# Filler matmuls of ones from the start, four sign buffers and earlier loads in a top-k attention and expert kernel

## The chip, the cores and the metric

The kernel runs on one core of a Trainium2 chip. The core has a matrix engine (TensorE, PE in the rows; its weight loads are listed as PEld), VectorE (DVE), ScalarE (ACT), GpSimd (POOL) and SyncE (SP), which here issues nearly all transfers. The metric is the device time of one execution in microseconds, lower is better.

## The reference

Attention over 2 batches, 8 heads, 576 tokens and 64 columns, in which each row keeps its 32 largest scores, and behind it a layer of 8 experts: each token goes to one expert, of which each takes at most 288.

```python
scores = scale * np.matmul(q, k.transpose(0, 1, 3, 2))
kth = np.partition(scores, -top_k, axis=-1)[..., -top_k:-top_k + 1]
scores = np.where(scores >= kth, scores, -1000000000.0)
attn = np.exp(scores - np.max(scores, axis=-1, keepdims=True))
attn = attn / (np.sum(attn, axis=-1, keepdims=True) + 1e-09)
x = np.matmul(attn, v)                       # then heads side by side: 1152 tokens x 512
expert_idx = np.argmax(x @ w_gate, axis=1)   # probs = softmax, gate_w = probs of that expert
h = np.maximum(np.einsum('ecd,edf->ecf', disp, w1), 0.0)
y = np.einsum('ecf,efd->ecd', h, w2)
out[i] = gate_w[i] * y[expert_idx[i], pos[i]]   # for tokens within capacity
```

## The kernel before

Attention is cut into 36 units: 9 tiles of 128 tokens by 4 pairs of heads. A unit goes through a pipeline in which each engine works on another unit at the same time. The order on each engine is the order of the code; nothing reorders it.

For unit `u` the steps are these. `scores` (L292, PE) writes two PSUM tiles that exist once, so the scores of the next unit wait until the unit before has been read. `heads` (L310 to L314, DVE) takes the eight largest of each of eight segments per head, sixteen MAX8, and the row maximum `mx` (L313). `shift` (L356, ACT) moves the scores, with the maximum taken off, from PSUM to `sm`; with it the PSUM tiles come free. `merge` and `bound` (L323 to L350, DVE) give a first bound for the 32nd value. `sign` (L365, ACT) writes the signs of `sm` against that bound to `sg` and counts them; `turn` (L372, POOL) multiplies `sm` by `sg` into `z`; `select` (L395 to L402, DVE) takes the eight largest of `z` and with the count the exact 32nd value. `penalty` (L411, ACT), `probs` (L430 to L432, PE and ACT) and `values` (L452, L455, PE) give the output. After each fourth unit the tile is routed (`route`, L518 to L561): logits on PE (L527), copied by DVE (L538), and an indirect transfer to the experts' buffer `xbuf`.

`sign_turn` writes, for one unit, the sign of head 0, work listed for ACT, the sign of head 1, and then the two products on POOL. The pool of the attention tiles has two buffers of each name, and a unit takes two of `sg`.

The q and k of a pair of heads are loaded by `load_qk` (L104, SP), split into a high and a low half in float16 (`split_qk`, L212 to L218) and transposed, `q` also with the halves swapped. For the first batch PE transposes (L244, L247), and ACT or DVE copies the result out (L252, L254). For the second batch POOL splits, and SP issues transposing DMAs (`trans_dma`, L233) and the swap (L223). The lists `side`, `mid`, `end` say at which of the pipeline's rounds such a step is issued; the loop at L1278 enters, for each pair, the load two rounds ahead of its split. SP issues its transfers in order: what stands behind a transfer that waits is issued after it. `init_xbuf` (L185) zeroes `xbuf` in six transfers from the same queue.

`warm` issues matmuls whose result is never read: `COLD` of them with 512 columns at the start, and four groups of 128 columns (`EARLY`) in the first three rounds. They multiply `identb` (weights) by `onesb`. The experts follow attention: weights are loaded, split in two halves and multiplied on PE.

Of the kernel before, what the change touches and what calls it, by code (L numbers as in the profile page):

```python
# [20 lines left out]
BF = mybir.dt.bfloat16  # L21
# [13 lines left out]
def kernel(  # L35
# [11 lines left out]
    nc = tc.nc  # L47
    B, H, S, D = q.shape
# [10 lines left out]
    consts = ctx.enter_context(tc.tile_pool(name="consts", bufs=1))  # L59
# [17 lines left out]
    def att(*a, **k):  # L77
        return P["att", 0].tile(*a, **k)
# [20 lines left out]
    def load_qk(b, p, tag="nat", names="qk"):  # L99
        for name in names:  # L100
            src = q if name == "q" else k
            XN[name, b, p] = x = (work.tile if tag == "nat" else att)([PR, 2, R, D], FT, name=name + "nat", tag=tag, bufs=4 if tag == "nat" else 2)
            for j in range(2):
                nc.sync.dma_start(x[:, j], bass.AP(  # L104
                    tensor=src.tensor, offset=src.offset + (b * H + 2 * p + j) * S * D,
                    ap=[[D, PR], [PR * D, R], [1, D]]))
# [16 lines left out]
    def load_v(b, js):  # L123
        for j in js:
# [4 lines left out]
            for c in range(4):  # L129
                nc.sync.dma_start(VM[b][:, c, :, j, 0:D],  # L130
                                  bass.AP(tensor=v.tensor, offset=o + (TAIL * j + c * 128) * D,
                                          ap=[[D, 128], hs, [1, D]]))

    load_qk(0, 0)
    load_qk(0, 1)
    load_qk(0, 2, "z")
# [11 lines left out]
    identb = consts.tile([128, 128], BF)  # L148
# [4 lines left out]
    nc.vector.tensor_copy(identh, ident)  # L153
    tri = consts.tile([128, 128], BF)
    nc.vector.tensor_scalar(tri, jp, 0.0, None, op0=OP.is_gt)
    onesb = consts.tile([128, 128], BF)
    nc.vector.memset(onesb, 1.0)
    zero = consts.tile([128, Dm + 2], FT)
    nc.vector.memset(zero[:, :Dm + 1], 0.0)
    nc.vector.memset(zero[:, Dm + 1:Dm + 2].bitcast(I32), 1 << 20)  # L160
# [197 lines left out]
    SEL, SG = {}, {}  # L358

    def sign(u, js=(0, 1)):  # L360
        if 0 in js:
            SG[u] = [att([128, S], BF, name="sg") for j in range(2)]
        for j in js:
            c = u * 2 + j
            nc.scalar.activation(SG[u][j], SM[u][:, j], AF.Sign, bias=VAL[u][0][:, 2, j:j + 1],  # L365
                                 scale=-(1.0 - 2.0 ** -20), accum_out=CNT[:, c:c + 1])
# [8 lines left out]
    def sign_turn(u, act, pool):  # L375
        sign(u, (0,))
        for f, *a in act:
            f(*a)
        sign(u, (1,))
        turn(u, js=(0,))  # L380
        if u < NU - 3:
            for f, *a in pool:
                f(*a)
        turn(u, js=(1,))
        if u == NU - 3:
            for f, *a in pool:
                f(*a)
# [96 lines left out]
    def tail_p():  # L484
        TAIL_P[:] = four()
# [435 lines left out]
    RANK = tuple(range(E))  # L921
    LEAST = 128

    COLD = 7
    EARLY = 30, 10, 30, 16
    FUSED = 3, 31

# [106 lines left out]
    def warm(n, few=False):  # L1034
        o = pv[:, 384:] if few else TAIL_P[2]
        x = onesb if few else onesb[:, None, :].to_broadcast([128, 4, 128])
        for i in range(n):
            nc.tensor.matmul(o, identb, x, start=True, stop=True)

    def attention(side, early, late, mid, pads, act, pool, end):  # L1040
        nc.vector.memset(OHS, 0.0)
# [84 lines left out]
        for st in range(3):  # L1126
            bound(L - 1, st)
        sign(L - 1)
        turn(L - 1)
        run(rt(T - 2, 1.5))  # L1130
# [106 lines left out]
    swap_psum(None, "bk")  # L1237
    tail_p()
    warm(COLD)
    for i in range(2):  # L1240
        split_qk(0, 0, i, ACT, DVE, tag="sm")
# [5 lines left out]
    for i, j, sw, o, eng in ((0, 0, 0, 0, ACT), (0, 1, 0, 1, ACT), (0, 0, 2, 3, DVE), (1, 0, 0, 4, ACT),  # L1247
# [13 lines left out]
    side, early, late, mid, pads = {}, {}, {}, {}, {}  # L1261
    act, pool, end = {}, {}, {}
    side[0] = [(warm, EARLY[0], True), (trans_qk, 0, 2, 0, ACT, 0)]
    mid[0] = [(trans_qk, 0, 2, 0, ACT, 1), (split_qk, 0, 3, 0, POOL, POOL, None, "pT"),
              (split_qk, 0, 3, 1, ACT, POOL, None, "pT")]
    end[0] = [(split_qk, 0, 2, 1, ACT, DVE, 2), (trans_qk, 0, 2, 1, ACT), (warm, EARLY[1], True)]
    side[1] = [(trans_qk, 0, 3, 0, ACT, 0)]
    mid[1] = [(trans_qk, 0, 3, 0, ACT, 1), (sign, 0), (turn, 0), (trans_qk, 0, 3, 1, DVE, 0), (warm, EARLY[2], True),
# [9 lines left out]
    for p in range(HP):  # L1278
        for i in range(2):
            at = 3 + 3 * (2 * p + i) // 2  # L1280
            if i == 0 and p:
                side.setdefault(at - 2, []).append((load_qk, 1, p))
            for part in range(3):
                side.setdefault(at + part // 2, []).append((split_qk, 1, p, i, POOL, POOL, part))
            side.setdefault(at + 1, []).append((trans_qk, 1, p, i, None))
# [13 lines left out]
    for n, (e, i, c) in enumerate(halves):  # L1299
        at = 18 + 3 * n  # L1300
# [108 lines left out]
```

## Time and profile before

| | us |
|---|---|
| median of 3 runs | 357.69 |
| lowest, highest | 357.67, 358.92 |
| the profiled execution | 359.89 |
| its span (first to last instruction) | 358.1 |
| attention, about | 12 to 233 |
| experts, about | 260 to 352 |

A row of a timeline gives the start and the length in us, the engine, the line, the operation, what it writes and reads, and how many instructions it stands for; in brackets the idle time of the engine before it and what ended it. PEclk is the granted clock of TensorE as a share of the full one.

### The profile page before, as it was taken

The numbers are of one execution on the slowest core, as the hardware profiler recorded it, in microseconds if no ns is written. First come the engines' busy times: TensorE is split into PE (matmuls) and PEld (weight loads), VectorE is DVE, ScalarE is ACT, GpSimd is POOL, SyncE is SP. The second block draws the span as 40 slices with busy tenths as digits, with TensorE's granted clock in tenths as the row PEclk, the third lists the DMA queues.
The fourth block names the chain that finished last, engine by engine and source line by source line (L and its number), as shares of the span: only waits on it lengthen the run. The fifth ranks groups of instructions, "written<-read, shape, count | busy, mean of one in ns | idle before, by whom it ended". The sixth has DMA issues, their size and how long they took to land. (4 is left out here: it accounts for less than half of the span.)

```text
span 358.1 us, 9808 instructions
## 1 busy us (share of the span) xinstructions
PE 318.2 (89%) x3356; PEld 264.4 (74%) x3361; DVE 310.9 (87%) x1607; ACT 283.0 (79%) x496; POOL 234.1 (65%) x270
## 2 busy tenths in 40 slices
PE   6986888897898998988889899999899999999991
PEld 3764776786786776777768788986446999996581
DVE  5899999999999999999999999886846959799930
ACT  4889999998979999999899998872266756886720
POOL 3967959599896798999999999592211020329321
PEclk9989999999999999999999999999999999999997
DMA  9739969686286910000301644504389999999900
GB/s 168 133 86 196 227 174 266 167 184 133 44 251 215 330 59 0 34 2 30 119 1 52 182 183 88 210 29 148 91 254 386 214 359 367 323 389 337 248 26 25
DMA packets 69921, 60.25 MB, mean 168 GB/s; under 512 B 52069, under 2 KB 52069, under 8 KB 69863
## 3 DMA queue, kind: packets, MB, share of 16 engines
q1 hardware_dynamic: 67719, 54.79, 56.8%
q0 software_dynamic: 1616, 4.73, 4.1%
q8 instruction: 28, 0.46, 0.6%
q14 instruction: 30, 0.25, 0.2%
q10 hardware_dynamic: 528, 0.02, 0.1%
HBM read 40.66 MB, written 12.09 MB: 147 GB/s over the span
## 5 line engine op out<-in xcount | busy, mean ns | idle before, releaser
L310 DVE MAX8 un<-s 128x8 f32<-128x72 f32 (+2 forms) x576 | 101.7, 224 | 3.1 <-PE s L292 3.0
L372 POOL TENSOR_TENSOR z<-sm,sg 128x576 f32<-128x576 f32 x71 | 89.4, 1280 | 7.6 <-ACT sg L365 7.2
L455 PEld LDWEIGHTS pV<-vm,pT 128*128 128x128 f32 (+1 forms) x640 | 71.3, 181 | 6.7 <-issue 3.3
L679 POOL DMA_INDIRECT out_dram<-y,xp x12 | 25.2, 2104 | 75.5 <-DVE y L846 39.1
L455 PE MATMUL pV<-vm,pT 128*128 128x65 f32 (+1 forms) x640 | 72.4, 261 | 0.0
L620 DVE TENSOR_TENSOR ws<-wr,ws 128x1024 bf16<-128x1024 f32 x54 | 64.9, 1250 | 2.8 <-ACT ws L614 2.6
L365 ACT ACTIVATE sg<-sm,mx 128x576 bf16<-128x576 f32 x72 | 55.4, 775 | 5.7 <-POOL z L372 5.6
L356 ACT ACTIVATE sm<-s,mx 128x576 f32<-128x576 f32 (+2 forms) x108 | 54.8, 582 | 5.7 <-DVE mx L313 5.6
L614 ACT ACTIVATE ws<-wr 128x2048 f16<-128x2048 f32 (+1 forms) x27 | 49.6, 1845 | 7.5 <-issue 4.4
L292 PE MATMUL s<-qk 128*128 128x512 f16 (+3 forms) x320 | 43.2, 291 | 12.1 <-ACT sm L356 12.0
L430 PE MATMUL p<-ident,sm 128*128 128x128 f32 x252 | 48.5, 281 | 6.0 <-ACT xT L524 5.5
L411 ACT ACTIVATE pen<-sm,nk 128x576 bf16<-128x576 f32 x71 | 51.6, 783 | 2.1 <-DVE nk L402 1.8
L398 DVE MAX8 z<-z 128x8 f32<-128x576 f32 x72 | 50.8, 747 | 0.0
L659 PEld LDWEIGHTS <-ws 128*128 128x128 f16 (+1 forms) x768 | 48.7, 98 | 1.2 <-issue 0.4
L431 PE MATMUL p<-identB,pen 128*128 128x128 bf16 x252 | 44.6, 220 | 4.9 <-ACT pen L411 4.8
L430 PEld LDWEIGHTS p<-ident,sm 128*128 128x128 f32 x252 | 36.1, 143 | 10.1 <-ACT xT L524 6.8
L431 PEld LDWEIGHTS <-pen 128*128 128x128 bf16 x324 | 33.5, 105 | 7.8 <-ACT pen L411 7.7
L292 PEld LDWEIGHTS <-qk 128*128 128x128 f16 (+1 forms) x320 | 20.4, 105 | 23.0 <-issue 14.5
L432 ACT ACTIVATE pT<-p 128x1152 f32<-128x1152 f32 x28 | 32.0, 1145 | 0.0
L620 POOL TENSOR_TENSOR ws<-wr,ws 128x1024 bf16<-128x1024 f32 x10 | 21.4, 2136 | 0.0
L831 PEld LDWEIGHTS <-ws 128*128 128x128 f16 (+1 forms) x288 | 21.3, 98 | 0.0
L659 PE MATMUL pT<-xe,ws 128*128 128x128 f16 (+5 forms) x312 | 19.6, 222 | 0.0
(271 smaller groups left out, 624.0 us busy)
## 6 DMA issues: line engine op xcount, KB each, us to landing
wr<-in_moe_w_dram SPq DMA_DIRECT2D x32, 1024.0 KB, 8.0
xbuf<-zero SPq DMA_DIRECT2D x6, 771.0 KB, 4.7
qnat<-in_q_dram SPq DMA_DIRECT2D x16, 144.0 KB, 3.9
knat<-in_k_dram SPq DMA_DIRECT2D x16, 144.0 KB, 3.1
out_dram<-zero SPq DMA_DIRECT2D x3, 768.0 KB
vm<-in_v_dram SPq DMA_DIRECT2D x16, 128.0 KB, 3.7
qk<-qk SPq DMA_DIRECT2D x14, 144.0 KB, 3.1
vt<-in_v_dram SPq DMA_DIRECT2D x4, 64.0 KB, 3.4
```

What stands on the lines that cost most here:

```text
L292: nc.tensor.matmul(PS[u][a][row:row + n, o:o + w], QK[b][2 * i][:, h, s:s + n], QK[b][1][:, h, c:c + w], start=(i == 0), stop=(i == 1))
L310: nc.vector.max(out=un[:, j, i], in_=segment(u, j, i))
L356: nc.scalar.activation(SM[u][:, j, o], i, AF.Identity, bias=VAL[u][0][:, 0, j:j + 1], scale=-1.0)
L365: nc.scalar.activation(SG[u][j], SM[u][:, j], AF.Sign, bias=VAL[u][0][:, 2, j:j + 1], scale=-(1.0 - 2.0 ** -20), accum_out=CNT[:, c:c + 1])
L372: engs[j].tensor_tensor(out=Z[u][:, j], in0=SM[u][:, j], in1=SG[u][j], op=OP.mult)
L398: nc.vector.max(out=z8[:, step - 1], in_=Z[u][:, step - 1])
L411: eng.activation(o, x, AF.Relu, bias=n)
L430: nc.tensor.matmul(pt[:, i], sm[:, cs], ident, start=True, stop=False, is_transpose=True)
L431: nc.tensor.matmul(pt[:, i], pen[:, cs], identB, start=False, stop=True)
L455: nc.tensor.matmul(PV[t][row:row + n, h0 + half], PT[u][:, 5 * half + c, row:row + n], VM[b][:, c, p, half], start=False, stop=(half == 1 ...
L620: eng.tensor_tensor(out=w[:, 1].bitcast(BF)[:, s], in0=r[:, s], in1=w[:, 0, s], op=OP.subtract)
L659: nc.tensor.matmul(o, a(i), c(i), start=(i == 0 and m == 0), stop=(i == k - 1 and m == 2))
```

## The change

`onesb` is written before the first loads instead of behind the constants, the fillers take it as both operands, `COLD` goes from 7 to 15, `sg` gets four buffers, and in the rounds in which a pair of the second batch is loaded, the load is put ahead of the other entries of that round instead of behind them.

```diff
+    onesb = consts.tile([128, 128], BF)
+    nc.vector.memset(onesb, 1.0)
     load_qk(0, 0)
...
     tri = consts.tile([128, 128], BF)
     nc.vector.tensor_scalar(tri, jp, 0.0, None, op0=OP.is_gt)
-    onesb = consts.tile([128, 128], BF)
-    nc.vector.memset(onesb, 1.0)
...
     def sign(u, js=(0, 1)):
         if 0 in js:
-            SG[u] = [att([128, S], BF, name="sg") for j in range(2)]
+            SG[u] = [att([128, S], BF, name="sg", bufs=4) for j in range(2)]
...
-    COLD = 7
+    COLD = 15
...
-            nc.tensor.matmul(o, identb, x, start=True, stop=True)
+            nc.tensor.matmul(o, onesb, x, start=True, stop=True)
...
             if i == 0 and p:
-                side.setdefault(at - 2, []).append((load_qk, 1, p))
+                side.setdefault(at - 2, []).insert(0, (load_qk, 1, p))
```

On VectorE, at the start of the program, the constants stood in this order before (`jp` comes from GpSimd, `ident` is the identity, `identb` its bfloat16 copy):

```order
L143 MEMSET act 1x1
L147 TENSOR_SCALAR ident<-jp 128x128
L149 CAST identb<-ident 128x128
L151 TENSOR_SCALAR identB<-ident 128x128
L153 CAST identh<-ident 128x128
L155 TENSOR_SCALAR tri<-jp 128x128
L157 MEMSET onesb 128x128
```

and stand so now:

```order
L135 MEMSET onesb 128x128
L145 MEMSET act 1x1
L149 TENSOR_SCALAR ident<-jp 128x128
L151 CAST identb<-ident 128x128
L153 TENSOR_SCALAR identB<-ident 128x128
```

The ones moved from the seventh place to the first, ahead of everything that waits for `jp`.

On SyncE, in the rounds in which pairs 1 and 2 of the second batch are loaded, this stood in the queue before (`hl` are split operands that GpSimd writes, one number for each; `qnat` and `knat` the loads, `xbuf` the zeroing):

```order
L185 DMA xbuf<-zero 128x3x514
L233 DMA_TRANSPOSE qk<-hl_718 128x6x96 x2
L223 DMA qk<-qk 64x1152 x2
L104 DMA qnat<-in_q_dram 96x6x64 x2
L104 DMA knat<-in_k_dram 96x6x64 x2
L185 DMA xbuf<-zero 128x3x514
L233 DMA_TRANSPOSE qk<-hl_819 128x6x96 x2
L185 DMA xbuf<-zero 128x3x514 x2
L233 DMA_TRANSPOSE qk<-hl_1034 128x6x96 x2
L223 DMA qk<-qk 64x1152 x2
L104 DMA qnat<-in_q_dram 96x6x64 x2
L104 DMA knat<-in_k_dram 96x6x64 x2
```

and this stands there now:

```order
L104 DMA qnat<-in_q_dram 96x6x64 x2
L104 DMA knat<-in_k_dram 96x6x64 x2
L185 DMA xbuf<-zero 128x3x514
L233 DMA_TRANSPOSE qk<-hl_726 128x6x96 x2
L223 DMA qk<-qk 64x1152 x2
L185 DMA xbuf<-zero 128x3x514
L233 DMA_TRANSPOSE qk<-hl_833 128x6x96 x2
L185 DMA xbuf<-zero 128x3x514
L104 DMA qnat<-in_q_dram 96x6x64 x2
L104 DMA knat<-in_k_dram 96x6x64 x2
L185 DMA xbuf<-zero 128x3x514
L233 DMA_TRANSPOSE qk<-hl_1042 128x6x96 x2
```

Each group of four loads moved ahead of the transposes and the swap that it followed. The order on ScalarE and on GpSimd is the same in both kernels.

## Rows read from the trace of the kernel before

**Rows 1.** The page, busy time and share of each engine.
```profile
PE 318.2 (89%) x3356; PEld 264.4 (74%) x3361; DVE 310.9 (87%) x1607; ACT 283.0 (79%) x496; POOL 234.1 (65%) x270
```
**Rows 2.** Busy time by stretch: length, then PE, PEld, DVE, ACT, POOL, clock, DMA.
```profile
12.26:84.50 72.24, 60.43 (x591) 49.95 (x590) 70.73 (x473) 66.79 (x127) 58.76 (x58) 0.98 0.84 177
84.50:233.00 148.50, 134.70 (x1381) 115.08 (x1381) 143.57 (x963) 138.53 (x279) 132.22 (x161) 1.00 0.36 113
260.00:322.00 62.00, 60.99 (x774) 54.90 (x774) 47.14 (x53) 43.41 (x49) 9.32 (x7) 1.00 1.06 329
```
**Rows 3.** Waits of DVE, 12 to 232 us: total, times, longest.
```profile
DVE un L310 <- PE s L292: 3.0, 5, 1.1
DVE r L538 <- PE pV L527: 1.2, 3, 0.5
```
**Rows 4.** Timeline of DVE in the prologue.
```profile
0.79 0.06 DVE L143 MEMSET act<- 1x1 f32 x1 [0.79 <-PEq L1392]
2.84 0.17 DVE L157 MEMSET onesb<- 128x128 bf16 x1
10.19 0.95 DVE L218 SCALAR_TENSOR_TENSOR hl<-knat,hl 96x768 f16<-96x768 f32 x1
12.26 2.33 DVE L310 MAX8 un<-s 128x8 f32<-128x72 f32 x16 [1.10 <-PE s L292]
17.36 0.24 DVE L310 MAX8 un<-s 128x8 f32<-128x72 f32 x1 [0.39 <-PE s L292]
21.91 0.24 DVE L310 MAX8 un<-s 128x8 f32<-128x72 f32 x1 [0.51 <-PE s L292]
```
**Rows 5.** Timelines of ACT and DVE around two later waits.
```profile
81.50 0.78 ACT L365 ACTIVATE sg<-sm,mx 128x576 bf16<-128x576 f32 x1 [1.18 <-POOL z L372]
85.23 0.24 DVE L310 MAX8 un<-s 128x8 f32<-128x72 f32 x1 [0.49 <-PE s L292]
200.95 0.77 ACT L365 ACTIVATE sg<-sm,mx 128x576 bf16<-128x576 f32 x1 [0.79 <-POOL z L372]
211.06 0.24 DVE L310 MAX8 un<-s 128x8 f32<-128x72 f32 x1 [0.48 <-PE s L292]
```
**Rows 6.** Timeline of PE in the prologue.
```profile
3.06 3.15 PE L1038 MATMUL bk<-onesb,identb 128*128 128x512 bf16 x7 [3.06 <-DVE onesb L157]
6.63 1.14 PE L244 MATMUL pT<-identh,hl 96*128 96x96 f16 x12 [0.43 <-DVE hl L218]
10.96 2.12 PE L292 MATMUL s<-qk 128*128 128x512 f16 x8
13.84 2.43 PE L1038 MATMUL pV<-onesb,identb 128*128 128x128 bf16 x30
16.10 0.68 PE L244 MATMUL pT<-identh,hl 96*128 96x96 f16 x12
16.61 1.15 PE L292 MATMUL s<-qk 128*128 128x512 f16 x8
19.12 0.95 PE L244 MATMUL pT<-identh,hl 96*128 96x96 f16 x12 [0.29 <-ACT qk L252]
```
**Rows 7.** Busy time by stretch; the last but two is the granted clock.
```profile
22.00:25.00 3.00, 3.00 (x30) 2.72 (x29) 2.86 (x22) 2.48 (x7) 1.40 (x2) 0.50 0.37 84
```
**Rows 8.** Timelines of ACT and POOL in the prologue.
```profile
14.90 1.52 ACT L356 ACTIVATE sm<-s,mx 128x576 f32<-128x576 f32 x3
12.83 1.64 POOL L216 TENSOR_TENSOR hl<-qnat,hl 96x768 f16<-96x768 f32 x1
```
**Rows 9.** Waits of ACT, 12 to 232 us.
```profile
ACT sg L365 <- POOL z L372: 5.6, 11, 1.2
```
**Rows 10.** Waits of POOL there, then timelines of SP and POOL.
```profile
POOL hl L214 <- DMA qnat<-in_q_dram: 6.1, 2, 3.4
48.26 1.20 SPq L104 DMA_DIRECT2D qnat<-in_q_dram  x2
70.03 0.83 POOL L214 TENSOR_SCALAR hl<-qnat 96x768 f16<-96x768 f32 x1 [3.42 <-DMA qnat<-in_q_dram]
```

## The prediction

> **What bounds the kernel now.** I read the page's engine table first, then the busy time by stretch, then VectorE's waits, and last the timelines around those waits. The page [rows 1] names no bound: PE has 89% and DVE 87%, averaged over stages that differ. By stretch [rows 2] they come apart. From 84.50 to 233.00 us DVE is busy 143.57 of 148.50 us, and from 12.26 to 84.50 us 70.73 of 72.24: attention runs at DVE's pace, and a gain there has to be an idle moment of DVE. From 260 to 322 us PE is busy 60.99 of 62.00: the experts run at PE's pace, on work that is released by the end of attention. I see there no transfer with a clock time of its own, so I let a shift of the end of attention pass through one for one.
>
> DVE's idle moments from 12 to 232 us are few [rows 3]. 3.0 us in five pieces are waits of the first maximum of a unit (L310) for the scores: the rows with the wait in brackets stand at 12.26 (1.10), 17.36 (0.39) and 21.91 (0.51) [rows 4], and at 85.23 (0.49) and 211.06 (0.48) [rows 5]. Another 1.2 us in three pieces are waits of the routing step L538 for its logits. What the change can take away is in these two lists.
>
> **Why the first three waits are there.** In the prologue PE works at the lower of its two clock levels. The seven fillers of 512 columns take 3.15 us, 0.45 us each, and 0.43 with the drain of the last left out, and the first scores take 2.12 us for eight matmuls; the second scores, the same eight, take 1.15. Twelve transposes take 1.14 us at 6.63 and 0.68 at 16.10 [rows 6]. The column of the granted clock reads 1.00 there and is no help; it shows a fall only later, 0.50 from 22 to 25 us [rows 7]. Before 13.84 the clock did not rise, although the seven fillers ran from 3.06 on; it rose during the thirty fillers at 13.84 (2.43 us, 81 ns each; a quarter of 0.43 us is 107 ns, the price at the lower level, and half of that, 54, the price at the upper).
>
> **Part one, the fillers.** The ones are now the first thing DVE writes, at 0.79 instead of 2.84 us [rows 4], and the fillers need no identity any more, which itself waits for GpSimd. They start when the 0.17 us of that memset are over, near 1.0 us by the same lag as the row of 3.06 has behind 2.84. There are 15 instead of 7. At the lower level all the way they would take 15 x 0.43 = 6.45 us and end at 7.45; the transposes behind them in PE's order are ready at 6.63. If the clock rises on the way, say at 5 us, nine are done by then and six go at half the price: end near 6.3, no delay.
>
> What a clock that is up by 7.5 us is worth I follow along DVE. Transposes and scores shrink by about 0.46 us per dozen and 0.97 us per eight scores. But DVE does not wait for PE alone: its split of the second k runs from 10.19 for 0.95 us and waits for GpSimd's and the loads' pace, not PE's, so the first maximum cannot start before 11.16 [rows 4]. The gain at the first maximum is therefore bounded by the idle of **1.10 us**, and I take all of it: before, 12.26 - 10.96 = 1.30 us passed from the start of the scores to the maximum; half of that behind 10.19, when the copies ahead of the split are over, is 10.84. At the second maximum (17.36, idle 0.39) the scores waited for the transposes at 16.10, which stood behind the thirty fillers, and for the shift of ACT, which ends at 14.90 + 1.52 = 16.42 [rows 6, 8]. With DVE 1.10 earlier the shift ends at 15.32; the thirty fillers, at the upper level, take 30 x 54 ns = 1.6 us; the transposes have their operand from GpSimd at 12.83 + 1.64 = 14.47 [rows 8] and go then. All three fit DVE being ready at 15.88, so the 0.39 goes if the clock holds until then and stays if it doesn't: I take half, **0.20**. The third idle moment (0.51) is the chain maximum, shift, scores of the loop itself and stays. Below, the bound of this part is a loss: the fillers end at 7.45, the clock has not risen, and all behind them is 0.82 us late. Above it is 1.10 + 0.39 + 0.51 = 2.00. The 86 later fillers of 128 columns keep their number; that their weights are ones and no identity I cost at nothing: the load of the weights is the same 128 columns, and they stand where PE waits anyway.
>
> **Part two, four sign buffers.** ACT's sign step (L365) waits for GpSimd's product (L372), which still reads the two buffers: 5.6 us in eleven pieces [rows 9]. Most of it dies on ACT, since DVE does not wait. Two places reach DVE. At 81.50 ACT waited 1.18 us; the shift follows it, then the scores, then DVE with 0.49 at 85.23. At 200.95 ACT waited 0.79, and DVE 0.48 at 211.06 [rows 5]. The first I take whole, **0.49**, because the wait on ACT is over twice as long and nothing else is late there. Of the second I take half, **0.24**: eight microseconds lie between, and PE's extra work of a first-expert quarter in them may be the cause by itself. Bounds: 0 (DVE is late for another reason) and, above, 0.97 plus the waits of L538 that stand behind ACT's late stretches, for which I allow two of the three, 0.8 us, as an estimate from the 1.2 in [rows 3]. No instruction is added. ACT running ahead is bounded by DVE's maximum, so nothing new can queue behind it; GpSimd gets its signs earlier in the same order.
>
> **Part three, loads ahead of transposes.** SP's queue is in order. The loads of pairs 1, 2 and 3 of the second batch stood behind transposing DMAs that wait for GpSimd's split, so GpSimd waited for its operand twice, 6.1 us in all, the second time 3.42 at 70.03; the loads behind the first wait were issued from 48.26 [rows 10]. Now four loads go first, 2.4 us of issue on SP (1.20 for the two of q, as much again for k); what they push back is a zeroing of the routing buffer and transposes that were waiting for GpSimd, and no one waits for either before the second batch. DVE shows no idle in either place, so the direct gain is **0**. Indirectly GpSimd is some 6 us less behind when it comes to 81.50, which is the same 0.49 as in part two; it counts once. Bounds: 0 and, below, 0.3 us, one idle moment of the size of those above, if a load meets the loads of v in the DMA engines.
>
> **The sum.** 1.10 + 0.20 + 0.49 + 0.24 = 2.03 us. The profiled execution took 359.89 us, its span 358.1; the median of the runs is 357.69, 0.6% less, and a shift of 2 us is the same in both. 357.69 - 2.03 = **355.7 us**. Half a percent, 1.8 us, is about what a measurement of this kernel can tell from no change.
>
> **The rivals.**
> *The clock falls back before the first scores.* Between the fillers and the scores PE has almost only transposes, six groups from 6.63 to the scores at 10.96. In the trace they never came with a rise: the clock stayed low through all of them, and it was low again from 22 us, after a stretch with a dozen transposes at 19.12, idle time and one set of scores [rows 6, 7]. Then the scores cost 2.12 us again; from 10.5 (transposes half gained) the first maximum comes at 11.8 instead of 11.16, the thirty fillers are slow as before, and the prologue gives 0.45 to 0.75 instead of 1.30. With the 0.73 of part two: 357.69 - 1.3 = 356.4.
> The Trainium skill, "TensorE: Matmul & The Clock Gate", in its part on the transpose on TensorE, says that a transpose does not engage the full clock as a matmul does; by that rule this rival would be the forecast, at 356.4. The trace agrees that transposes alone left the lower level in place, and shows nothing on whether they lose a level that fillers have reached; I give the rule a quarter.
> *The steady stretch gives nothing.* The buffers and loads take the waits off ACT and GpSimd, and DVE finds its next wait 0.1 us further on; only the prologue stays: 357.69 - 1.30 = 356.4.
> *Slower: the fillers stand in the way.* PE works in order. If the clock has not risen when the transposes are ready at 6.63, the rest of the fillers is paid in full: 0.82 us, and the thirty at 13.84, if they miss the rise that they had before, cost 3.2 instead of 2.43, another 0.8. Loss 1.6, less the 0.73 of part two: 358.6. It decides at one point, the clock at 6.6 us. Against it: the fillers now run more than twice as long without a break as the seven that failed.
>
> **How the numbers follow.** Forecast 0.50, clock falls back 0.25, steady stretch gives nothing 0.13, fillers in the way 0.12. The forecast alone reaches from 354.4 (1.49 + 0.97 + 0.8 = 3.26 gained) to 356.1 (1.10 + 0.49). The range goes down to that 354.4 and up to 358.0, inside the slower case. Faster by over half a percent means under 355.9: 0.43 of the 0.50, with 0.06 from the two middle cases, 0.49. Slower by as much, over 359.5, needs the last case and a steady stretch that gives nothing: 0.07. The rest, 0.44, is within.
>
> **What would show it.** Fillers from about 1.0 us, and among them a spacing that drops from 0.43 to half; twelve transposes at 6.6 us in under 0.8 us; first scores in some 1.2 us, first maximum near 11.2. ACT's sign step with no wait for GpSimd's product at all. GpSimd's two waits for q gone. DVE's idle of 0.49 near 84 gone. The prediction is wrong if the first maximum stays near 12.2, or if DVE leaves attention 2 us earlier and the end does not move: then a transfer in the experts had a time of its own.

## The result and the profile after

The changed kernel takes **356.01 us** in the median of 13 executions, the kernel before 359.31 in 13 on the same chip: a ratio of 0.992 with a 95% interval of 0.9892 to 0.9949, faster by 0.5 to 1.1 percent, which is 1.8 to 3.9 us. The forecast was 355.7, with a gain of 2.03. The time came out close to it, and the gain forecast lies in the interval, near its lower end. Between the medians it is 3.3 us; the kernel before took longer here than in the three runs that the forecast started from. Single executions of the kernel before lie further apart (357.05 to 364.63) than those of the changed one (355.45 to 357.85), and the ratios leave out the disturbed ones; that is why ratios are compared below, and not single times.

The profiled execution of the changed kernel took 356.31 us, with a span of 354.4 where the kernel before had 358.1. Its page, busy time and share of each engine, answers to [rows 1]:

```profile
PE 317.9 (90%) x3364; PEld 261.8 (74%) x3369; DVE 310.6 (88%) x1607; ACT 283.1 (80%) x496; POOL 233.3 (66%) x270
```

Nothing is to be seen there. By stretch (columns as in [rows 2]) DVE is a little busier in both parts of attention, 71.05 and 144.32 us instead of 70.73 and 143.57, and PE in the experts, 61.48 instead of 60.99. The last line answers to [rows 7]: the lower clock is still there, five microseconds later.

```profile
12.26:84.50 72.24, 60.61 (x591) 49.00 (x588) 71.05 (x475) 68.83 (x131) 61.52 (x60) 0.98 0.86 184
84.50:233.00 148.50, 135.99 (x1394) 116.36 (x1396) 144.32 (x965) 140.15 (x280) 132.78 (x163) 1.00 0.34 111
260.00:322.00 62.00, 61.48 (x783) 55.71 (x779) 49.11 (x56) 44.12 (x49) 11.58 (x7) 1.00 1.10 341
...
27.00:28.00 1.00, 1.00 (x7) 0.45 (x5) 0.96 (x9) 0.83 (x2) 1.00 (x2) 0.50 0.91 206
```

PE's timeline in the prologue answers to [rows 6]. Fifteen fillers start at 1.06 and take 5.70 us, less than the 6.45 that the lower level all the way would cost; the transposes behind them take 0.68 instead of 1.14, the first scores 1.15 instead of 2.12.

```profile
1.06 5.70 PE L1038 MATMUL bk<-onesb 128*128 128x512 bf16 x15 [1.06 <-DVE act L145]
6.59 0.68 PE L244 MATMUL pT<-identh,hl 96*128 96x96 f16 x12
...
10.15 1.15 PE L292 MATMUL s<-qk 128*128 128x512 f16 x8
```

On DVE (timeline, answers to [rows 4]) the first maximum starts at 11.18 without a wait; the third, at 21.91 before, at 20.74 with the same wait of 0.51; and L466, the last normalisation of attention, stands at 230.47:

```profile
11.18 0.23 DVE L310 MAX8 un<-s 128x8 f32<-128x72 f32 x1
...
20.74 0.24 DVE L310 MAX8 un<-s 128x8 f32<-128x72 f32 x1 [0.51 <-PE s L292]
...
230.47 0.16 DVE L466 TENSOR_SCALAR rs<-pV 128x4 f32<-128x4 f32 x1 [0.86 <-PE pV L455]
```

DVE's waits from 12 to 232 us (total, times, longest; answers to [rows 3]): one of the five waits for scores is left, 0.5 of 3.0 us, and the waits of L538 for logits have shrunk from 1.2 to 0.9. The same view of the kernel before has a third line, which [rows 3] does not show, and it is gone altogether; L952 is a small matmul that counts tokens, right behind the logits on PE. First the line of before, then the changed kernel:

```profile
DVE r L538 <- PE pV L952: 0.6, 2, 0.4
```

```profile
DVE r L538 <- PE pV L527: 0.9, 3, 0.4
...
DVE un L310 <- PE s L292: 0.5, 1, 0.5
```

In this trace the wait of ACT's sign step for GpSimd's product [rows 9] and GpSimd's two waits for q [rows 10] do not occur.

**Where the 3.7 us between the two spans lie.** I cut each trace at two rows of DVE: the start of the third maximum (21.91 and 20.74) and L466 (233.76, a row of the trace of before with the same form, and 230.47). Up to the third maximum the changed kernel gains 1.17 us, from there to L466 2.12 (211.85 against 209.73), behind it 0.41 (124.34 against 123.93). The forecast put 1.30, 0.73 and 0 there.

### The profile page after: what moved, and what is told of

It is laid out like the page before. It is cut to its first block, busy times and chain, and to the rows that moved or that the text cites. A ratio compares the mean times of both kernels' runs of the same rounds, so it can differ in the third digit from the quotient of the medians.

```text
span 354.4 us, 9822 instructions
## 1 busy us (share of the span) xinstructions
PE 317.9 (90%) x3364; PEld 261.8 (74%) x3369; DVE 310.6 (88%) x1607; ACT 283.1 (80%) x496; POOL 233.3 (66%) x270
## 5 line engine op out<-in xcount | busy, mean ns | idle before, releaser
L310 DVE MAX8 un<-s 128x8 f32<-128x72 f32 (+2 forms) x576 | 101.8, 225 | 0.7 <-PE s L292 0.5
L372 POOL TENSOR_TENSOR z<-sm,sg 128x576 f32<-128x576 f32 x71 | 89.4, 1278 | 11.1 <-ACT sg L365 10.7
L679 POOL DMA_INDIRECT out_dram<-y,xp x12 | 24.4, 2034 | 75.5 <-DVE y L846 40.2
L614 ACT ACTIVATE ws<-wr 128x2048 f16<-128x2048 f32 (+1 forms) x27 | 49.5, 1845 | 6.3 <-issue 4.9
L398 DVE MAX8 z<-z 128x8 f32<-128x576 f32 x72 | 50.9, 748 | 0.0
```

The lines of the kernel that those rows point to most:

```text
L310: nc.vector.max(out=un[:, j, i], in_=segment(u, j, i))
L372: engs[j].tensor_tensor(out=Z[u][:, j], in0=SM[u][:, j], in1=SG[u][j], op=OP.mult)
L614: nc.scalar.activation(w[:, 0, s], r[:, s], AF.Copy)
```

## The experiments

The theory was that of the forecast: what the change removes from DVE's waits is the gain, fillers most of it. The rival, after the first runs: the clock at the start is a matter of the single execution, so the fillers gain little on average, and buffers and loads carry the change. Every kernel below also has one profiled execution, cut at the same two rows; *third* is the start of the third maximum, *steady* the time from it to L466, *rest* from L466 to the end of the span, *weights* what ACT's split L614 waited there for a transfer of weights from 300 us on, *fall* a stretch near 220 us at the lower clock. The profiled execution of e8 took 364.00 us, where its other six took 356.84 to 357.68, so its *rest* is not typical of that kernel.

| kernel | ratio to before, interval | third | steady | rest | weights | fall |
|---|---|---|---|---|---|---|
| before | | 21.91 | 211.85 | 124.34 | 1.6 | no |
| changed | 0.992, 0.9892 to 0.9949 | 20.74 | 209.73 | 123.93 | 0 | no |
| changed, again (e5) | 0.9868, 0.9819 to 0.9917 | 20.68 | 212.49 | 124.23 | 0 | yes |
| fillers (e1) | 1.0004, 0.9947 to 1.0062 | 21.10 | 212.28 | 123.52 | 0 | yes |
| signs (e2) | 0.9953, 0.9915 to 0.999 | 21.36 | 209.69 | 127.95 | 5.4 | no |
| loads (e3) | 0.9965, 0.9925 to 1.0005 | 20.64 | 214.10 | 124.66 | 1.0 | yes |
| signs, loads (e4) | 0.9884, 0.9828 to 0.994 | 21.97 | 209.57 | 123.56 | 0 | no |
| signs, loads (e8) | 0.9896, 0.9849 to 0.9943 | 21.04 | 210.88 | 130.28 | 6.9 | yes |
| signs, loads, no first fillers (e6) | 0.9899, 0.985 to 0.9947 | 21.66 | 209.62 | 123.72 | 0 | no |
| fillers, signs (e7) | 0.9919, 0.9879 to 0.996 | 20.75 | 211.44 | 124.81 | 2.8 | no |
| changed, reads moved (f1) | 0.9916, 0.9881 to 0.9951 | 21.30 | 209.97 | 123.83 | 0 | no |
| changed, small fillers (f2) | 0.9891, 0.9836 to 0.9945 | 21.34 | 211.01 | 126.75 | 4.1 | yes |
| before, both of these (f3) | 0.9974, 0.994 to 1.0009 | 21.55 | 211.71 | 124.64 | 3.0 | no |
| changed, both of these (f4) | 0.9901, 0.9859 to 0.9944 | 21.12 | 210.16 | 123.32 | 0.4 | no |

e1 to e4 ran on one chip, e5 to e8 on another, f1 to f4 on a third. On these the kernel before took 361.37, 362.56 and 361.13 us in the median.

**e1: part one alone.**

```diff
+    onesb = consts.tile([128, 128], BF)
+    nc.vector.memset(onesb, 1.0)
     load_qk(0, 0)
...
-    COLD = 7
+    COLD = 15
...
-            nc.tensor.matmul(o, identb, x, start=True, stop=True)
+            nc.tensor.matmul(o, onesb, x, start=True, stop=True)
```

> Only part one: ones first, both operands ones, 15 fillers. Theory (the parts add): the clock rises among the fillers, the first maximum stands near 11.2 us and the second near 15.9, DVE's idle of 1.10 and 0.39 is gone, ACT's 5.6 us of waits for the product stay, time 1.5 us (0.4%) under before. Rival (the gain needs the steady stretch): the prologue gains and a later wait gives it back, time within 0.5 us of before.

361.88 us against 361.37: no gain that could be seen, with an interval of about 2 us to either side. The start looks as forecast (first scores 1.15, no wait at the first two maxima), though a little later than expected (11.65 and 16.57 us); ACT's waits for the product stayed, 4.2 us in ten pieces. But in this execution the clock fell near 220 us, and DVE's wait at L552 was 2.1 us instead of 0.5:

```profile
DVE r L552 <- PE pV L548: 2.1, 1, 2.1
```

**e2: part two alone.**

```diff
-            SG[u] = [att([128, S], BF, name="sg") for j in range(2)]
+            SG[u] = [att([128, S], BF, name="sg", bufs=4) for j in range(2)]
```

> Only part two: four sign buffers. Theory: ACT's waits for the product vanish, DVE's idle of 0.49 near 85 and 0.48 near 211 and about 0.9 of its waits on the routing logits go, first maximum stays at 12.3, time 1.9 us (0.5%) under before. Rival (the late loads are the cause of what GpSimd owes): GpSimd's waits for q stay, its products come as late as before and DVE keeps at least half of the idle, time under 1 us below before.

359.27 us; by the ratio 1.7 us less than the kernel before, with an interval of 0.4 to 3.1. The theory had 1.9. DVE's waits from 12 to 232 us are those of the changed kernel, line for line (three of five are shown), though GpSimd still waits 2.2 us for q and 2.9 us in its second wait at that place, as the rival had it:

```profile
DVE r L538 <- PE pV L527: 0.9, 3, 0.4
DVE rs L466 <- PE pV L455: 0.9, 1, 0.9
DVE un L310 <- PE s L292: 0.5, 1, 0.5
```

So is the steady stretch: 209.69 us against 209.73 for the changed kernel and 211.85 before. **With four buffers alone 2.16 us are gone from it in this execution.** The idle moments that are gone are the two of [rows 5] (0.49 and 0.48), two waits of L538 for the logits of a tile (0.37 at 99.11 and 0.25 at 194.34 in the trace of before), 0.26 of a third (0.46 at 123.65) and 0.10 at 109.58: 1.95 in sum. Of DVE's waits 0.29 is new (0.20 at L372, 0.09 more at L466), and DVE's busy time in the stretch is 0.44 us shorter (205.24 instead of 205.68), for which I know no reason. One of the moments that are gone, in the timeline of DVE before:

```profile
99.11 0.17 DVE L538 COPY r<-pV 128x8 f32<-128x8 f32 x1 [0.37 <-PE pV L952]
```

Which of them are the buffers' the other traces tell: before, e1, e3 and f3 have two buffers, the other ten have four. The wait of L310 near 211 us is 0.48 to 0.51 in all of the four and in none of the ten; the wait of L538 near 123 us is 0.46 in all of the four and 0.19 to 0.21 in the ten. L538 waits near 99 us in two of the four (0.36 and 0.37) and near 194 us in three (0.22 to 0.33), and in none of the ten. But the wait of L310 near 85 us is in the trace of before alone: e1, e3 and f3 have two buffers and do not have it. Without a fall of the clock and without waits for GpSimd's product, the steady stretch is 211.85 and 211.71 us with two buffers (before, f3) and 209.57 to 210.16 with four (six traces): about 2 us.

L538 hangs on the sign buffers through PE. Its logits stand in PE's order behind scores, scores behind ACT's shift, and the shift behind the sign step. A timeline of PE in the trace of before, at the scores that follow the wait of 81.50 in [rows 5]:

```profile
84.48 1.17 PE L292 MATMUL s<-qk 128*128 128x512 f16 x8 [1.76 <-ACT sm L356]
```

and the same scores in e2:

```profile
82.70 1.17 PE L292 MATMUL s<-qk 128*128 128x512 f16 x8 [0.49 <-ACT sm L356]
```

PE waits 1.27 us less. It is 91% busy in this stretch (134.70 of 148.50 us), and what it is late here it carries to the logits. That the logits at 99.11 are late because of this wait is argued from the order, not measured apart; f3 has the wait near 99 us without one near 85.

This execution also had the longest *rest* but one. That is taken up below.

**e3: part three alone.**

```diff
-                side.setdefault(at - 2, []).append((load_qk, 1, p))
+                side.setdefault(at - 2, []).insert(0, (load_qk, 1, p))
```

> Only part three: loads ahead of the transposes. Theory: GpSimd's 6.1 us of waits for q go, ACT's wait of 1.18 near 81 goes with them and DVE's 0.49 near 85, but ACT's waits from 99 us on stay at about 4 us, time 0.5 us (0.1%) under before. Rival (loads are the cause): ACT's waits for the product fall under 1 us in all and the time by 1.9 us.

359.2 us, ratio 0.9965, with an interval that just reaches 1. GpSimd's waits for q are gone, and of DVE's idle moments that of 85.23 (which e1 and f3, with the loads late, do not have either); that of 211.06 stays, with 0.49 at 210.64. ACT still waits 3.3 us in eight pieces for the product, near the 4 of the theory and not under the 1 of the rival. The clock fell twice in this execution, between 106 and 114 and between 222 and 226 us, so its steady stretch cannot be compared.

**e4: parts two and three.** Both edits above.

> Parts two and three without the fillers. Theory: as four sign buffers alone, 1.9 us (0.5%) under before, the loads add nothing that DVE sees; first maximum at 12.3. Rival: clearly under the sign buffers alone, by 0.5 us or more.

356.58 us, ratio 0.9884: 1.2% under the kernel before, with an interval of 0.6 to 1.7. The two parts alone had 0.9953 and 0.9965, 0.8% in sum, which the interval takes in. It is 2.5 us under the buffers alone, on the side of the rival, though the intervals of e2 and e4 overlap. With the fillers unchanged this is already about the time of the changed kernel.

**e5 to e8: the fillers again, and the loads beside the signs.** e5 is the changed kernel, e8 is e4 again; e6 differs from e8 by

```diff
-    COLD = 7
+    COLD = 0
```

and e7 from e5 by `append` in place of `insert(0, ...)` for the load.

> The changed kernel once more, beside the three below. Both theories: 1.8 to 4 us under the kernel before. Theory 1 (the early fillers are a term of the gain): 0.5 to 1.5 us under the kernel with signs and loads alone. Theory 2 (the early fillers only make sure of what the seven late ones reach in some executions anyway): within 0.5 us of it.

> Signs and loads without the change of the fillers, again, on the chip of the changed kernel. Theory 1: 0.5 to 1.5 us above the changed kernel. Theory 2: within 0.5 us of it, and its executions lie as close together.

> Signs and loads as in the changed kernel, and no filler at the start at all. Theory 1: the clock stays at its lower level through the first transposes and scores, the first maximum waits 1 us or more, and the time is 1 to 2 us above the changed kernel. Theory 2: the same picture at the first maximum, but under 0.5 us of it reaches the end.

Medians 356.27 (e5), 357.39 (e8) and 357.11 (e6). By its ratio e5 is 4.8 us under the kernel before, more than the 1.8 to 4 that both theories named. The fifteen early fillers are worth 1.1 us against the seven late ones here, inside what theory 1 named, and 0.8 against none, between the two theories; four of the six executions of e5 (from 355.75 on) are below every one of e8 and e6 (from 356.77 on). The intervals of the ratios overlap, so this is likely rather than shown. The seven late fillers gain nothing that could be seen against none.

What they do to the clock the traces do show. Without fillers, in e6, the first transposes and scores run like this (timeline of PE):

```profile
6.48 1.14 PE L244 MATMUL pT<-identh,hl 96*128 96x96 f16 x12 [6.48 <-DVE hl L218]
...
10.80 1.73 PE L292 MATMUL s<-qk 128*128 128x512 f16 x8
```

The clock rises in the scores themselves, and the first maximum waits 0.85 us. With seven late fillers it differs by execution. In e2 it is up at 6.56 and down again at 9.71 and in the scores:

```profile
6.56 0.68 PE L244 MATMUL pT<-identh,hl 96*128 96x96 f16 x12 [0.46 <-DVE hl L218]
...
9.71 1.14 PE L244 MATMUL pT<-identh,hl 96*128 96x96 f16 x12 [0.62 <-DVE hl L218]
10.65 2.12 PE L292 MATMUL s<-qk 128*128 128x512 f16 x8
```

The first scores took 2.12 us in before, e2 and e4, 1.63 in f3, 1.15 in e3 and e8, and the wait at the first maximum was 1.10, 0, 0.61, 0.75, 0 and 0: 0.41 in the mean of these six. With the fifteen it was 0 and the scores took 1.14 or 1.15 in all seven traces; which of their three differences does it, the earlier start, the number or the ones as weights, no run separates. The start of the third maximum says the same: 21.41 in the mean of the six, 21.00 of the seven, **0.41 us earlier**; with a spread of 1.33 us among the six and 0.66 among the seven, this is a rough figure. At the second maximum DVE waited in two of the six (0.39 and 0.38) and in one of the seven (0.28). The Trainium skill, "TensorE: Matmul & The Clock Gate", in Part 1 on the clock gate, says that the number of matmuls that run slowly at the start differs from run to run; the trace agrees, with 2.12, 1.63 and 1.15 for the same scores behind the same fillers.

The upper level did not last in every trace with fifteen fillers. In f1 and f4 it was lost ahead of the third scores, which took 2.08 us instead of 1.17, and the wait at the third maximum was 1.02 us instead of 0.51. From f4, timelines of PE and of DVE:

```profile
19.85 2.08 PE L292 MATMUL s<-qk 128*128 128x512 f16 x8 [0.70 <-ACT sm L356]
```

```profile
21.12 0.24 DVE L310 MAX8 un<-s 128x8 f32<-128x72 f32 x1 [1.02 <-PE s L292]
```

> The changed kernel without part three: loads again behind the transposing transfers. If the loads are worth something of their own beside the sign buffers: 0.5 us or more above the changed kernel, or executions spread over several microseconds, with transfers in the experts that PE waits for. If not, as I costed it: within 0.3 us of the changed kernel, GpSimd again waiting for q near 48 and 70 us and nothing of it on VectorE.

358.62 us; by the ratios 1.8 us more than e5, with intervals that overlap, so I had likely priced the loads too low; the fastest executions differ by 0.5 (356.26 and 355.75). In e7 GpSimd waits longer for q than it did before [rows 10], and now DVE feels it. First GpSimd's waits, then DVE's, from 12 to 232 us:

```profile
POOL hl L214 <- DMA qnat<-in_q_dram: 7.2, 2, 3.7
```

```profile
DVE z L398 <- POOL z L372: 1.4, 4, 0.5
```

L398 reads the product of L372, which stands behind the waiting split on GpSimd; the four waits lie between 81 and 107 us, behind the split that started late, at 69.52. The steady stretch is 211.44, 1.7 more than the changed kernel's. The order of the loads is no sure cure, though: in e5, which has it, GpSimd waited 6.2 us for the transfers that read the operands split before, and DVE 1.1 us for its products, between 82 and 107 us (its longer steady stretch, 212.49, has the fall near 220 us in it as well):

```profile
POOL hl L214 <- DMA qk<-hl: 6.2, 4, 2.5
```

```profile
DVE z L398 <- POOL z L372: 1.1, 3, 0.5
```

And in e2, without it, GpSimd waited 5.1 us and DVE not at all. The cover over GpSimd's waits is thin: 5.1 us of them cost DVE nothing in e2 and 6.1 nothing in the trace of before, where DVE comes later for the products; 6.2 and 7.2 cost 1.1 and 1.4.

**f1 to f4: two suspects outside the change.** Two things lengthened single executions whatever the kernel: the fall of the clock near 220 us, in five of the fourteen traces, and the wait for weights in the experts. For the second there was a trail. SyncE reads from `order` which expert's weights to load next (L863), between two groups of loads. In e2 and e8, the two traces with the longest *rest*, one such read took 2.7 us (least, median and longest of the four, in ns; e2, then e8, then f1 below, in which they are moved):

```profile
L863 SPq TENSOR_LOAD <-order x4: 270/365/2692, 275.4 to 305.4; - x4
```

```profile
L863 SPq TENSOR_LOAD <-order x4: 268/364/2670, 276.3 to 306.8; - x4
```

```profile
L863 SPq TENSOR_LOAD <-order x4: 262/265/392, 263.9 to 265.7; - x4
```

In the other traces with the reads in their place the longest took 0.49 to 0.77 us. In e8 ACT's split then waited for seven groups of weights, from 317 us on (timeline of ACT, two of the seven rows):

```profile
324.49 1.91 ACT L614 ACTIVATE ws<-wr 128x2048 f16<-128x2048 f32 x1 [1.82 <-DMA wr<-in_moe_w_dram]
...
335.76 1.91 ACT L614 ACTIVATE ws<-wr 128x2048 f16<-128x2048 f32 x1 [1.81 <-DMA wr<-in_moe_w_dram]
```

f1 moves the reads:

```diff
-        load_x(3, 0, SIZES[3])
         check(0)
         check(1)
         count()
+        for e in range(4, E):
+            which(e)
+        load_x(3, 0, SIZES[3])
...
-                            which(e + 2)
-                            which(e + 3)
```

f2 puts small fillers where PE waits for ACT's shift ahead of scores:

```diff
+    HOLD = {5: 5, 6: 5, 7: 8, 8: 5, 9: 8, 10: 5, 13: 8, 14: 4, 17: 8, 18: 4, 21: 6, 25: 8, 26: 4, 28: 8, 29: 8,
+            30: 4, 35: 9}
...
+            run([(warm, HOLD[i + 1], True)] if i + 1 in HOLD else [])
             run(at(4, values, 0) + picks + at(-1, scores)
```

f3 is the kernel before with both, f4 the changed kernel with both.

> The changed kernel, with SyncE's four reads of the experts' order moved: not between the weight loads of the experts, but once, behind the count and ahead of the transposing load of expert 3. Theory A (the long executions come from two places outside the change's sums, the fall of PE's clock near 220 us and a read of the order that now and then takes 2.7 us and holds up the weight loads): no wait of ACT's split for weights from 300 us on, no execution over 359 us, median equal to the changed kernel or up to 0.7 us below. Theory B (the gain is the removed waits of VectorE and nothing else): as the changed kernel, 356.0 to 356.4, with an odd execution over 359.

> The changed kernel with 4 to 9 small fillers in 17 rounds of attention, where PE waits 0.3 to 0.5 us for ACT's shift ahead of the scores. Theory A: the granted clock stays at 1.00 from 30 to 230 us, the end of attention on VectorE comes at 230.5 to 231.5 us, median 0.3 to 1.0 us below the changed kernel. Theory B: clock as before or not, same time within 0.3 us.

> The kernel before with both of these edits and nothing of the change. Theory A: executions within 4 us of each other instead of 9, median 2 to 4 us below the kernel before, its fastest execution about as fast as the fastest of the kernel before (357.2). Theory B: the spread of 9 us stays and the median is within 1 us of the kernel before.

> The changed kernel with both edits. Theory A: median 355 to 355.8, executions within 1.5 us. Theory B: 356.0 to 356.4.

Medians 357.39 (f1), 357.13 (f2), 356.57 (f4), and f3 359.95 against 361.13 for the kernel before; the ratios of f1, f2 and f4 (0.9916, 0.9891, 0.9901) are those of the changed kernel within their intervals, and that of f3 reaches past 1. The changed kernel itself did not run on this chip, so the medians do not decide between the theories: those of f1 and f4 lie above what either named, and f3 is 1.2 us under the kernel before, between the two. No execution of f1 is over 359 us (the longest is 358.35), as theory A had it; of f4 two are (359.13 and 360.09), and f3 has one of 366.68, with the other eleven within 2.8 us. **Theory A falls in its part on the clock.** In f2 nine fillers close the last wait ahead of scores, 0.54 us in the changed kernel, to next to nothing, the clock falls all the same, and attention ends at 232.35. First PE in the changed kernel, then in f2 (timelines), then busy time by stretch in f2, the granted clock last but two:

```profile
214.10 1.17 PE L292 MATMUL s<-qk 128*128 128x512 f16 x8 [0.54 <-ACT sm L356]
```

```profile
212.75 0.67 PE L1040 MATMUL pV<-onesb 128*128 128x128 bf16 x9
...
214.57 1.17 PE L292 MATMUL s<-qk 128*128 128x512 f16 x8
```

```profile
218.00:220.00 2.00, 2.00 (x18) 2.00 (x17) 1.97 (x8) 1.42 (x3) 1.92 (x3) 0.86 0.70 131
220.00:222.00 2.00, 2.00 (x14) 1.60 (x15) 1.93 (x18) 0.58 (x2) 2.00 (x4) 0.50 0.82 170
```

Its part on the reads is not settled. With the reads moved no trace has a long read, and f1 and f4 wait 0 and 0.4 us for weights; but f3 waits 3.0 with the reads moved, and f2 4.1 with none over 0.53. So a long read is not the only thing that makes weights late, and what did it there I did not find. f4 had the shortest execution of all, 354.81; as a kernel it cannot be told from the changed one.

## Why the prediction was near, step by step

**Part one was mis-sized, and its size was that of one execution.** The mechanism came as written: fillers from 1.06 (forecast near 1.0), transposes in 0.68, first scores in 1.15, first maximum at 11.18 (forecast 11.16), no delay by the fillers. In these two traces it gave 1.17 us of the 1.30. But the wait of 1.10 at the first maximum, the largest term of the sum, was that of one trace: with the same seven fillers two of five others had one, of 0.61 and 0.75. Over six and seven traces the part is worth about 0.41; over the medians of e5 and e8, 1.1; in e1 nothing that could be seen. The 0.20 for the second maximum stands on a wait that four of the six traces with seven fillers do not have.

**The rival of the falling clock was the fate of the old fillers at the first scores; the new ones met it later.** In e2 and e4 the clock, once up, fell during the transposes and the first scores paid 2.12. The Trainium skill, "TensorE: Matmul & The Clock Gate", in Part 4 on the transpose, says that the full clock does not engage for transposes. The trace agrees in these two executions as far as the level was lost there, and disagrees in all seven traces with fifteen fillers, where the dozens of transposes of L244 ahead of the first scores take 0.68 or 0.69 us. The 0.51 at the third maximum stayed in five of these seven, as forecast; in f1 and f4, where the clock fell ahead of the third scores, it became 1.02, which no term of the sum and no rival had.

**Part two was too small by 1.4 us.** The steady stretch gained 2.12 us where the sum had 0.73. The step that failed is the bound: I counted two idle moments of L310, halved one, and left the waits of L538 to the upper bound. e2 shows the whole of both moments (0.97) and 0.98 more, 0.88 of it at L538. The 0.8 that the upper bound allowed for L538 was about its size, but by luck: it meant two of the three waits in [rows 3], of which two stayed (0.40 and 0.30) and one only shrank, and the 0.62 that went whole are the line on L952, which [rows 3] leaves out. They belonged in the sum, if the logits are late for the reason argued above. Nor were the two moments of L310 weighed rightly. The one taken whole, near 85 us, is in one of four traces with two buffers; the one halved, near 211 us, is in all four, and the four buffers remove it in all ten. (The "eight microseconds" there are 8.9 from the end of ACT's step to the start of DVE's wait.)

**Part three is likely not 0.** The direct gain was put at 0 because DVE showed no idle moment at either of GpSimd's waits. That nobody waits for the transposes that the loads push back was wrong: in e5 GpSimd's splits waited 6.2 us for transposes, though in the other trace of the same kernel not at all. e7 shows the price when that cover is gone, which I had not worked out: DVE frees 1 to 2 us, comes sooner for the products, and a GpSimd that waits 7.2 us is late for it by 1.4. By the ratios e3 alone gains 1.3 us and e4 2.5 over e2, with wide intervals, of which I can show the 1.4 in that one execution only.

**"No transfer with a clock time of its own" was wrong.** In some executions the weights have one. In the trace of before ACT waited 1.6 us for them, and the last part of the span gave 0.41 of the gain. In e2, e8 and f2 the *rest* is 126.75 to 130.28 us, where it is 123.32 to 124.23 in the seven traces with at most 0.4 of such waits. So a gain in attention can be lost in the executions in which the weights are late; that the 1.6 us made the 0.41 is argued, not shown.

The forecast's 355.7 thus came from a first term that was too large on average, a second and third that were too small, and a starting point, 357.69, that lay among the shorter times of the kernel before. That it came within 0.3 us of the measured time is luck: between the medians the gain was 1.3 us larger than forecast, and the start 1.6 us higher. The slower rival did not come: with fifteen fillers the first transposes started between 6.29 and 6.89 us in the seven traces, against 6.63 [rows 6]. In f1 and f4 they stood 0.3 and 0.4 us behind fillers with their operand ready, and no first maximum waited for it. Nor did the steady stretch give nothing: it gave the larger share.

## What to carry to other kernels

Read an idle moment that hangs on the clock in several executions before it goes into a sum; one trace can show the largest of what happens, or the smallest. When an engine's wait is removed, follow everything that stands behind the waiting instruction on the engines after it, the small steps too: here four waits of 0.1 to 0.4 us, three of them in the routing, made nearly half of what the buffers gave in one execution. And a wait that is in one trace of several is no price: of two that looked alike in the trace of before, 0.49 and 0.48 us, one belonged to that execution and the other to the kernel. An engine that waits unseen (GpSimd for its loads) is a debt that can come due when the one in front is made faster.

## What was unexpected of the hardware

The granted clock fell to 0.50 for three to four microseconds near 220 us in five of fourteen traces, with PE busy 1.74 to 2.00 of each 2 us in the fall and the four microseconds ahead of it, and in f2 with the wait ahead of the scores filled; DVE's wait at L552 was then 2.1 instead of 0.5 us, and the steady stretch 210.88 and 211.01 instead of 209.6 to 209.7 (e8 and f2 against the changed kernel, e2, e4 and e6). A read of one number by SyncE from `order` took 0.26 us at best and 2.7 in two executions. The clock also fell between 19 and 30 us in seven of the fourteen traces, with seven fillers and with fifteen. And the column of the granted clock reads 1.00 in the first microseconds of the trace of before although the first scores there take 2.12 us, 1.8 times the 1.15 of the next ones [rows 6]: at the start of a program the level is to be read from the lengths of equal instructions.
